# Attention and gated MLP on one core: later heads' scores in plain fp32 on half the array, p turned through DRAM

## The chip, the cores and the metric

The kernel runs on one core of a Trainium2 chip. The metric is the device time of one execution in microseconds; of several executions, the median. Engines are named as in the profile: PE is the tensor engine, DVE the vector engine, ACT the scalar engine, POOL GpSimd, SP the queue that issues most DMAs. PEld is PE's loading of weights.

## The reference

Banded attention with sink columns feeds a two-layer MLP with a cosine gate. Batch 4, 8 heads, 768 positions, head size 64; 3072 tokens of width 512, hidden width 2048. All in fp32.

```python
scores = scale * np.matmul(q, k.transpose(0, 1, 3, 2))
keep = is_sink | in_window                  # 4 sink columns, window 128
scores = np.where(keep, scores, -1000000000.0)
a = softmax(scores)                         # with 1e-9 in the denominator
x = np.matmul(a, v)                         # heads side by side: 3072 x 512
h = x @ w_in
out = (h * np.cos(h)) @ w_out
```

## The kernel before

The queries are cut into 12 chunks of 256 rows (two blocks of 128) of one batch, and a chunk has 8 heads. A query block needs the key block of its own rows and the one before, and 8 sink columns where it lies behind those (264 score columns in all). A chunk's attention output is the `x` of its MLP part: 8 slots per chunk, each with 24 matmuls at L458 (`h_mm`), the gate on ACT and DVE, and 12 matmuls at L518 (`out_mm`). Chunk 0 takes its second product in plain fp32 at L513. Elsewhere an fp32 operand is split in a rounded high part and a low part, both in the type fp32r, and the products hi\*lo, hi\*hi and lo\*hi are summed. The weights come as 64-bit floats and are put together on DVE early in the run (L579 to L621).

**Early heads** are the 24 heads of the first chunks of batches 0 to 2 (`NEH`). Their q and k are turned by PE (L862), the scores are plain fp32 matmuls with a pair of heads on the two halves of the rows (`scores_pe`, L882), p is turned by PE (`turn`, L1057), and the values are plain fp32 on the two halves of the columns (`values_pe`, L1110).

**Later heads** are the other 72 (64 of chunks behind a batch's first, 8 of batch 3's first). k is loaded twice, on partitions 0 to 63 and 64 to 127 (`load_k`, L813), and turned by DVE (`k_turn`, L911); the sink columns are appended (`k_sink`); k is split by `k_hi` (ACT, L923) and `k_lo` (DVE, L929), q by `q_hi` and `q_lo` (L898, L905) with the high part on one half of the partitions and the low part on the other. `scores` (L938) is two fp32r matmuls per head and query block, one with the high and one with the low part of k. `mask` (L951) moves the scores to SBUF with the mask added, then come exponential, `lap` (which folds the two key blocks), and `norm`. `turn` transposes p on PE (L1053, two 128x128 blocks; in batch 3's first chunk three, L1057); `p_hi` and `p_lo` split it (L1070, L1079), `part` on POOL separates the two key blocks again (L1092), and `values` multiplies (L1132).

PSUM has one bank `s` for scores and one `tp` for turns. At the start, the limits (window and sink count) come by ACT's queue, `limits` and `mask_0` to `mask_2` make three masks on DVE, and `beyond` tests whether the limits fit.

What sets the order: every step is entered in a `Plan` with the engines it may use, its estimated duration, the steps and buffers it waits for and a priority from the table `C`. `Plan.place` runs this list forward and back and fixes the engine and the place of each step; `emit` writes the instructions in that order, and each engine's queue keeps it. In gaps of PE before the first `out_mm`, `fill` puts matmuls on an unused tile (`idle`, L1411). So another number in `C` moves instructions all over the program.

Of the kernel before, what the change touches and what calls it, by code (L numbers as in the profile page):

```python
# [16 lines left out]
P = 128  # L17
# [10 lines left out]
C = {  # L28
# [7 lines left out]
}  # L36
TN, TV, TW = (230.0, 2.5), (128.0, 3.0), 1.7
BEGIN = {"PE": 3.4, "ACT": 0.7, "POOL": 2.6, "DVE": 2.3, "SP": 0.8}
MIN_TOP = 1.125 * 2.0**-15
# [11 lines left out]
class Plan:  # L51
# [12 lines left out]
    def __init__(self):  # L64
        self.steps, self.bufs, self.port, self.lock, self.hold, self.skew, self.more, self.trip = [], {}, set(), set(), set(), set(), {}, {}

# [5 lines left out]
    def add(self, engines, fn, deps, prio, table=None, port=False, lock=False, hold=True, more=0.0, skew=False, trip=1.7):  # L72
# [11 lines left out]
        self.more[i], self.trip[i] = more, trip  # L84
        return i

    def lap(self, i, e):
        return -0.025 if i in self.skew and e in ("ACT", "DVE") else self.OVERLAP[e]
# [144 lines left out]
def attn_moe_kernel(ctx, tc, q, k, v, n_sink, window, w_in, w_out, out):  # L233
# [45 lines left out]
    rel, col = rc[:, 0], rc[:, 1]  # L279
    nw_i = cp.tile([P, 2, 2], I32, name="nw_i")  # L280
# [9 lines left out]
    def setup():  # L290
# [17 lines left out]
        nc.vector.tensor_copy(out=rc, in_=rc_i)  # L308
        nc.vector.tensor_reduce(
# [4 lines left out]
    def load_limits(e):  # L314
        nc.scalar.dma_start(out=nw_i[:, 0, :], in_=n_sink.unsqueeze(0).broadcast_to([P, 2]))
        nc.scalar.dma_start(out=nw_i[:, 1, :], in_=window.unsqueeze(0).broadcast_to([P, 2]))
        nc.scalar.activation(out=flag[:, 2:3], in_=quarter[0:1], func=AF.Exp)

    def limits(e):
        nc.vector.tensor_copy(out=nw4, in_=nw_i)  # L320
        nc.vector.tensor_single_scalar(out=neg, in_=nw4[:, :, 0], scalar=0.0, op=ALU.is_lt)
# [4 lines left out]

    def beyond(e):
# [386 lines left out]
    def banded_path():  # L714
# [8 lines left out]
        diag, prev, cols = mb[:, SW:], mb[:, :P], ma[:, :P]  # L723
        vs = env.vs = ap.tile([P, H // GQ, GQ, 2, D], F32R, name="vs")
# [3 lines left out]
        def masked(m):  # L728
            nc.vector.tensor_scalar(out=m, in0=m, scalar1=-1.0, scalar2=MASKED, op0=ALU.add, op1=ALU.mult)

        def mask_0(e):
            nc.vector.tensor_scalar(out=diag, in0=rel, scalar1=wd_f, scalar2=None, op0=ALU.is_lt)
            nc.vector.scalar_tensor_tensor(out=diag, in0=rel, scalar=0.0, in1=diag, op0=ALU.is_ge, op1=ALU.mult)
            nc.vector.tensor_scalar(out=cols, in0=col, scalar1=ns_f, scalar2=None, op0=ALU.is_lt)
            nc.vector.tensor_tensor(out=m0, in0=cols, in1=diag, op=ALU.max)
            masked(m0)

        def mask_1(e):
            nc.vector.tensor_copy(out=mb[:, P:SW], in_=cols[:, :NSINK])
            nc.vector.tensor_scalar(out=prev, in0=rel, scalar1=float(P), scalar2=wd_f, op0=ALU.add, op1=ALU.is_lt)  # L740
            nc.vector.tensor_tensor(out=cols, in0=cols, in1=prev, op=ALU.max)
            nc.vector.tensor_copy(out=ma[:, P:], in_=diag)
            masked(ma)

        def mask_2(e):
            masked(mb)

        heads = []
        for a, (b, i0) in enumerate(chunks):
            for h in range(H):  # L750
# [12 lines left out]
                o.one = i0 > 0  # L763
                o.nw = [SW] * CB if o.one else o.w
# [5 lines left out]
        def load_batch_k(o):  # L770
            def fn(e):
                for dup in range(2):
                    for c in range(2):
                        nc.sync.dma_start(
                            out=o.xs[dup * 64 + c * 32 : dup * 64 + c * 32 + 32],
                            in_=k[o.b, :, 0:32, c * 32 : c * 32 + 32].rearrange("h s d -> s h d"),
# [12 lines left out]
        def batch_k(o):  # L789
            def fn(e):  # L790
                t = ap.tile([P, KB, SW], F32, name=f"tb_{o.tag}", tag="tk").rearrange("p n s -> p (n s)")[:, : H * 32]
                nc.vector.transpose(out=t, in_=o.xs.rearrange("p h s -> p (h s)"))
                o.ts = ap.tile([P, H, NSINK], F32, name=f"ts_{o.tag}", tag="ts")
# [840 lines left out]
```

## Time and profile before

| What | us |
|---|---|
| runs, median (lowest to highest, 3 runs) | 716.63 (716.15 to 719.03) |
| the profiled execution | 715.12 |
| its span | 713.4 |
| PE busy | 701.1 (98%) |
| DVE busy | 615.8 (86%) |
| ACT busy | 545.1 (76%) |
| POOL busy | 105.4 (15%) |

The span is from the first to the last instruction of the profiled execution, 1.7 us below its own time. The granted clock of PE is 1.00 in nearly the whole span. The DMA engines are busy 41% of it with the loads and stores of SP's queue. Busy time of PE counts a matmul from its start to its end, and matmuls overlap, so a group's sum of busy times may exceed the stretch that it takes.

### The profile page before, as it was taken

How to read it: one execution, taken by the hardware profiler on the slowest of the kernel's cores; microseconds unless marked ns; L12 is line 12 of the kernel's file. 1: busy time of each engine (PE TensorE's matmuls, PEld its weight loads, DVE VectorE, ACT ScalarE, POOL GpSimd, SP SyncE). 2: the span in 40 equal slices, each digit the busy share in tenths (PEclk: the TensorE clock that was granted, in tenths of full speed). 3: DMA queues.
4: the chain of work that ended last, by engine and by line, in shares of the span. 5: the costliest groups of instructions: out<-in, count | busy, mean ns of one | idle time of the engine just before them, and what ended most of it. 6: DMA issues, size and time to landing. Idle time of an engine off the chain costs nothing.

```text
span 713.4 us, 14956 instructions
## 1 busy us (share of the span) xinstructions
PE 701.1 (98%) x4780; PEld 622.7 (87%) x4780; DVE 615.8 (86%) x1766; ACT 545.1 (76%) x1349; POOL 105.4 (15%) x190
## 2 busy tenths in 40 slices
PE   8889999999999999999999999999999999999996
PEld 7676767989989999999999999999998999999995
DVE  7999999788999999999999998897798998875332
ACT  5989674488897988988978979878879788784431
POOL 1000000012122122221221221221010221212000
PEclk9999999999999999999999999999999999999999
DMA  6977762134644843843844532322332422100001
GB/s 171 255 230 218 216 181 66 30 50 124 176 95 99 216 104 87 227 104 61 226 93 102 122 52 47 77 40 48 84 53 47 86 50 40 47 12 8 31 1 33
DMA packets 215896, 71.48 MB, mean 100 GB/s; under 512 B 204288, under 2 KB 204800, under 8 KB 215808
## 3 DMA queue, kind: packets, MB, share of 16 engines
q1 hardware_dynamic: 215232, 70.17, 41.2%
q8 instruction: 40, 0.66, 0.4%
q14 instruction: 48, 0.39, 0.2%
q10 hardware_dynamic: 576, 0.26, 0.1%
HBM read 64.10 MB, written 6.29 MB: 99 GB/s over the span
## 4 chain that ended last, share of the span: by engine, by line
PE 93%; DVE 6%; issue 0%; ACT 0%; POOL 0%; POOLq 0%; DVEq 0%
PE h L458 38%; PE acc L518 34%; PE av L1132 6%; PE s L938 5%; PE acc L513 4%; PE tp L1053 2%; DVE p L951 1%; PE tp L1057 1%; DVE w_in L585 1%; PE av L1110 1%; DVE w_in L591 1%; PE s L882 1%; PE idle L1411 1%; DVE lo_in L621 1%; PE gp L1037 0%
## 5 line engine op out<-in xcount | busy, mean ns | idle before, releaser
L458 PE MATMUL h<-xhi,lo_in 128*128 128x256 f32 x768 | 224.6, 292 | 0.2 <-DVE g L491 0.2
L458 PE MATMUL h<-xlo,hi_in 128*128 128x256 f32 x768 | 217.0, 283 | 0.0
L458 PE MATMUL h<-xhi,hi_in 128*128 128x256 f32 x768 | 216.9, 282 | 0.0
L458 PEld LDWEIGHTS h<-xhi,lo_in 128*128 128x128 f32 x768 | 146.2, 190 | 6.2 <-issue 1.6
L458 PEld LDWEIGHTS h<-xhi,hi_in 128*128 128x128 f32 x768 | 146.4, 191 | 4.1 <-issue 1.7
L458 PEld LDWEIGHTS h<-xlo,hi_in 128*128 128x128 f32 x768 | 146.3, 190 | 0.0
L518 PE MATMUL acc<-hi_out,ghi 128*128 128x512 f32 x350 | 142.4, 407 | 0.0
L518 PE MATMUL acc<-lo_out,ghi 128*128 128x512 f32 x350 | 137.6, 393 | 0.0
L518 PE MATMUL acc<-hi_out,glo 128*128 128x512 f32 x350 | 137.3, 392 | 0.0
L1092 POOL TENSOR_SCALAR_AFFINE_SELECT pz<-pz 128x512 fp32r<-128x512 f32 x128 | 83.1, 649 | 249.3 <-DVE pz L1079 230.4
L467 ACT ACTIVATE yt<-h 128x512 int32<-128x512 f32 x96 | 57.3, 597 | 51.0 <-PE h L458 50.0
L960 ACT ACTIVATE p<-p,st 128x264 f32<-128x264 f32 (+1 forms) x192 | 93.2, 488 | 0.2
L473 DVE SCALAR_TENSOR_TENSOR r<-h,yt 128x512 f32<-128x512 f32 x96 | 65.3, 681 | 26.0 <-ACT yt L467 25.8
L480 ACT ACTIVATE r<-r,neg 128x512 f32<-128x512 f32 x96 | 69.6, 725 | 21.6 <-DVE r L473 20.9
L951 DVE CUSTOM_DVE_ANT_0 p<-s,mk 128x264 f32<-128x264 f32 (+2 forms) x168 | 68.1, 405 | 12.6 <-PE s L938 8.9
L518 PEld LDWEIGHTS acc<-hi_out,glo 128*128 128x128 f32 x350 | 65.8, 188 | 14.8
L518 PEld LDWEIGHTS acc<-hi_out,ghi 128*128 128x128 f32 x350 | 66.1, 189 | 7.3
L518 PEld LDWEIGHTS acc<-lo_out,ghi 128*128 128x128 f32 x350 | 66.2, 189 | 7.0
L485 DVE TENSOR_TENSOR h<-h,r 128x512 f32<-128x512 f32 x88 | 60.9, 692 | 11.4 <-ACT r L480 10.8
L503 DVE TENSOR_TENSOR glo<-h,ghi 128x512 fp32r<-128x512 f32 x88 | 59.9, 680 | 12.0 <-ACT ghi L497 11.7
L497 ACT CAST ghi<-h 128x512 fp32r<-128x512 f32 x88 | 51.5, 585 | 24.5 <-DVE h L485 18.4
L938 PE MATMUL s<-r,l 128*128 128x264 f32 (+2 forms) x288 | 59.6, 289 | 0.0
(139 smaller groups left out, 1239.6 us busy)
## 6 DMA issues: line engine op xcount, KB each, us to landing
raw<-in_moe_w_in_dram SPq DMA_DIRECT2D x32, 512.0 KB, 4.5
raw<-in_moe_w_out_dram SPq DMA_DIRECT2D x32, 512.0 KB, 4.2
xk<-in_k_dram SPq DMA_DIRECT2D x256, 48.0 KB, 2.0
v<-in_v_dram SPq DMA_DIRECT2D x64, 96.0 KB, 2.2
out_dram<-raw SPq DMA_DIRECT2D x22, 256.0 KB, 3.1
xq<-in_q_dram SPq DMA_DIRECT2D x144, 32.0 KB, 1.9
v<-in_v_dram SPq DMA_DIRECT2D x32, 64.0 KB, 3.6
xq<-in_q_dram SPq DMA_DIRECT2D x24, 64.0 KB, 3.7
```

Of the source, the lines that this page charges most:

```text
L458: nc.tensor.matmul(out=o.h[:, t, :], lhsT=w[:, fs], rhs=xx[:, c, :], start=(c == 0 and n == 0), stop=(c == NC - 1 and n == 2),)
L467: nc.scalar.activation(out=yt, in_=o.h, func=AF.Copy, scale=INV2PI, bias=0.25)
L473: nc.vector.scalar_tensor_tensor(out=o.r, in0=o.h, scalar=INV2PI, in1=yt, op0=ALU.mult, op1=ALU.subtract)
L480: nc.scalar.activation(out=o.r, in_=o.r, func=AF.Sin, scale=TWOPI_DOWN, bias=quarter)
L485: nc.vector.tensor_tensor(out=o.h, in0=o.h, in1=o.r, op=ALU.mult)
L497: nc.scalar.copy(out=o.ghi, in_=o.h)
L503: e.tensor_tensor(out=o.glo, in0=o.h, in1=f32(o.ghi), op=ALU.subtract)
L518: nc.tensor.matmul(out=x.acc[j], lhsT=gg[:, t, j * P : (j + 1) * P], rhs=w, start=(f == 0 and n == 0), stop=(f == NFT - 1 and n == 2), ski ...
L938: nc.tensor.matmul(out=o.s_ps[j][:, :w], lhsT=o.l[:, j * P : (j + 1) * P], rhs=r.rearrange("p n s -> p (n s)")[:, c0 : c0 + w], start=(n = ...
L951: nc.vector.tensor_tensor_reduce(out=o.p[:, j, :w], in0=o.s_ps[j][:, :w], in1=masks[min(o.i0 + j, 2)][:, :w], op0=ALU.add, op1=ALU.min, sc ...
L960: nc.scalar.activation(out=o.p[:, j, :w], in_=o.p[:, j, :w], func=AF.Exp, bias=o.lead.st[:, 0, o.nth, j : j + 1], scale=-1.0, accum_out=o. ...
L1092: nc.gpsimd.affine_select(out=env.pz4[:, :, :, n], in_=f32(env.pz4)[:, :, :, 0], pattern=[[0, 2], [0, CB], [sign, P]], compare_op=ALU.is_g ...
```

## The change

- **Scores of later heads**: `load_k` brings the k of two heads, one on each half of the partitions, once. `k_turn` and `q_turn` serve a pair; `k_hi`, `k_lo`, `q_hi`, `q_lo` are gone. `scores` is one plain fp32 matmul per head and query block, two heads on the two halves of the rows; the second head's scores go to the bank `tp`. The sink keys are loaded and turned per pair.
- **p of later heads**: `turn` is left to the early heads. `p_blocks` has DVE turn p within blocks of 32x32 into `wt`; `p_store` writes it to a DRAM tile `dt` in 4 DMAs, `p_load` reads it back in 4 DMAs, so that the blocks land where the full transpose wants them (`pt`). `p_hi` and `p_lo` read `pt` from SBUF, and `p_lo` may go to POOL.
- **Early values**: `values_pe` takes a pair of heads in one step, alternating the two halves.
- **Masks**: `mask_0` to `mask_2` compare with the limits as loaded and multiply by the mask value at once; `limits` is one cast, and `beyond` with the rest of the old `limits` goes behind the masks of a later head. The first k load is halved between SP and ACT's queue, and the copy of the first turned q and k is in two steps. The loads of the sink keys and values wait for masks of head 8 and head 12.
- **The table `C`** and the cost constants are other numbers.

```diff
-    "AE": 17.984, "ALT": 0.863, "CK": 42.675, "DA": 1.14, ...
+    "AE": 14.238, "ALT": 0.313, "CK": 66.775, "DA": -2.106, ...
...
         def load_k(o):
             def fn(e):
-                for dup in range(2):
+                for h in range(2):
                     for c in range(2):
                         nc.sync.dma_start(
-                            out=o.xk[dup * 64 + c * 32 : dup * 64 + c * 32 + 32],
-                            in_=k[o.b, o.h, o.kb0 * P : (o.kb0 + o.nkb) * P, c * 32 : c * 32 + 32].rearrange(
+                            out=o.xk[h * 64 + c * 32 : h * 64 + c * 32 + 32],
+                            in_=k[o.b, o.h + h, o.kb0 * P : (o.kb0 + o.nkb) * P, c * 32 : c * 32 + 32].rearrange(
...
-        def scores(o, j):
-            def fn(e):
-                i, w = o.i0 + j, o.w[j]
-                o.s_ps[j] = ps.tile([P, 2, NT], F32, name=f"s_{o.tag}_{j}", tag="s").rearrange("p a b -> p (a b)")
-                c0 = max(i - 1 - o.kb0, 0) * o.sw
-                for n, r in enumerate((o.r1, o.r2)):
+        def scores(o, o1, j):
+            def fn(e):
+                w = o.w[j]
+                sa = ps.tile([P, 2, NT], F32, name=f"s_{o.tag}_{j}", tag="s").rearrange("p a b -> p (a b)")
+                sb = ps.tile([P, 4 * P], F32, name=f"s_{o1.tag}_{j}", tag="tp")
+                c0 = max(o.i0 + j - 1 - o.kb0, 0) * o.sw
+                for n, (oo, s_ps) in enumerate(((o, sa), (o1, sb))):
+                    oo.s_ps[j] = s_ps
+                    r = slice(n * D, (n + 1) * D)
                     nc.tensor.matmul(
-                        out=o.s_ps[j][:, :w], lhsT=o.l[:, j * P : (j + 1) * P],
-                        rhs=r.rearrange("p n s -> p (n s)")[:, c0 : c0 + w], start=(n == 0), stop=(n == 1),
+                        out=s_ps[:, :w], lhsT=o.tq[r, j * P : (j + 1) * P],
+                        rhs=o.tk[r].rearrange("p n s -> p (n s)")[:, c0 : c0 + w], start=True, stop=True,
                     )
...
+        def p_blocks(o, oe):
+            def fn(e):
+                if o is oe:
+                    o.wt = ap.tile([P, 2 * (CB + 1) * P], F32, name=f"wt_{o.tag}", tag="wt", bufs=WT)
+                flat = oe.wt[:, o.odd * o.nb * P : (o.odd + 1) * o.nb * P]
+                if o.one:
+                    nc.vector.transpose(out=flat.rearrange("p (j w) -> p j w", j=CB), in_=o.p[:, :, :P])
+                    return
+                for j, c0 in enumerate((0, o.w[0])):
+                    nc.vector.transpose(out=flat[:, c0 : c0 + o.w[j]], in_=o.p[:, j, : o.w[j]])
+            return fn
+
+        def p_store(oe):
+            def fn(e):
+                n = 2 * oe.nb
+                oe.dt = dp.tile([32, 2 * (CB + 1) * 4, 4, 32], F32, name=f"dt_{oe.tag}", tag="dt", bufs=DT)
+                src = oe.wt[:, : n * P].rearrange("p (g b) -> p g b", b=32)
+                for r in range(4):
+                    nc.sync.dma_start(out=oe.dt[:, : n * 4, r], in_=src[r * 32 : r * 32 + 32])
+            return fn
+
+        def p_load(oe):
+            def fn(e):
+                n = 2 * oe.nb
+                oe.pt2 = ap.tile([P, 2 * (CB + 1) * P], F32, name=f"pt_{oe.tag}", tag="pt2", bufs=PT)
+                src = oe.dt.rearrange("a (g c) r b -> c a g (r b)", c=4)
+                dst = oe.pt2.rearrange("p (g w) -> p g w", w=P)
+                for c in range(4):
+                    nc.sync.dma_start(out=dst[c * 32 : c * 32 + 32, :n], in_=src[c, :, :n])
+            return fn
...
-        i = add([("ACT", 5.2)], load_limits, [], -3000.0)
-        i = add([("DVE", 0.76)], limits, [i], -3000.0)
-        add([("DVE", 0.4)], beyond, [i], C["LB"])
-        mks = [add([("DVE", 1.4)], mask_0, [i], -3000.0, port=True)]
-        mks.append(add([("DVE", 1.15)], mask_1, mks[:], -2999.0, port=True))
-        mks.append(add([("DVE", 0.3)], mask_2, mks[1:], C["LB"], port=True))
+        lim = i = add([("ACT", 4.13)], load_first, [], -3000.0, ahead=1.0)
+        i = add([("DVE", 0.2)], limits, [i], -3000.0)
+        read = i
+        mks = [add([("DVE", 0.58)], mask_0, [i], -3000.0, port=True)]
+        mks.append(add([("DVE", 0.78)], mask_1, mks[:], -2999.0, port=True))
+        mks.append(add([("DVE", 0.15)], mask_2, mks[1:], C["LB"], port=True))
...
+            ts = []
+            for oo in (oe, o):
+                ts.append(
+                    add([("DVE", dve(oo.nb * P) + (0.02 if oo.one else 0.1))], p_blocks(oo, oe), oo.nm + (ts or [bwt]), t + DA + C["TB"] + 0.1 * oo.odd)
+                )
+                oo.bp.users.append(ts[-1])
+            i = add(dma(2.0), p_store(oe), [*ts, bdt], t + DA + C["TB"] + 1.0, more=205.0 * o.nb, trip=1.9)
+            bwt.users.append(i)
+            o.rd = add(dma(2.0), p_load(oe), [i, o.bpt], t + DA + C["TB"] + 2.5, more=140.0 * o.nb, trip=1.9)
+            bdt.users.append(o.rd)
```

On PE, among the slots of the MLP, one head's scores before: two fp32r matmuls of 264 columns into one bank (`r` are the parts of k, `l` those of q).

```order
L458 MATMUL h_1885<-xhi_721,hi_in_1138 128x256
L458 MATMUL h_1885<-xlo_748,hi_in_1138 128x256
L938 MATMUL s_2_4_1_1922<-r_0_2_4_1867,l_2_4_1864 128x264
L938 MATMUL s_2_4_1_1922<-r_0_2_4_1873,l_2_4_1864 128x264
L458 MATMUL h_1885<-xhi_721,lo_in_1176 128x256
L458 MATMUL h_1885<-xhi_721,hi_in_1158 128x256
```

After, for the same query block, the pair's two heads, in plain fp32 from `tk` and `tq` as they were turned:

```order
L468 MATMUL h_1905<-xhi_744,hi_in_1206 128x256
L468 MATMUL h_1905<-xlo_870,hi_in_1206 128x256
L931 MATMUL s_2_4_1_1940<-tk_2_4_1640,tq_2_4_1642 128x264
L931 MATMUL s_2_5_1_1941<-tk_2_4_1640,tq_2_4_1642 128x264
L528 MATMUL acc_0_1597<-hi_out_1265,ghi_1777 128x512
L528 MATMUL acc_0_1597<-lo_out_1560,ghi_1777 128x512
```

Four matmuls for a pair and block have become two, and they stand as one block between full matmuls; there are 72 such blocks.

On PE before, the turn of a later head's p stood between matmuls at L518:

```order
L518 MATMUL acc_0_2227<-hi_out_1011,ghi_2321 128x512
L518 MATMUL acc_0_2227<-lo_out_1446,ghi_2321 128x512
L518 MATMUL acc_0_2227<-hi_out_1011,glo_2330 128x512
L1053 MATMUL tp_2_4_2450<-ident,p_2_4_1892 128x128 x2
L518 MATMUL acc_1_2237<-hi_out_1011,ghi_2321 128x512
L518 MATMUL acc_1_2237<-lo_out_1446,ghi_2321 128x512
```

The changed order has no such rows for later heads.

On SP before, in a later stage: k loads of one head (x4), q, v, and weights for the check.

```order
L813 DMA xk_75<-in_k_dram 32x12x32 x4
L801 DMA xq_74<-in_q_dram 32x8x32 x4
L813 DMA xk_76<-in_k_dram 32x12x32 x4
L824 DMA v_77<-in_v_dram 128x3x64
L639 DMA raw_71<-in_moe_w_out_dram 128x1024
L774 DMA xq_73<-in_k_dram 32x8x32 x4
```

After, around one pair's round trip: `dt` is the DRAM tile, `pt` what comes back.

```order
L1072 DMA dt_2_4_3763<-wt_2_4_3707 32x16x32 x4
L839 DMA v_77<-in_v_dram 128x3x64
L557 DMA out_dram<-raw_72 128x512
L839 DMA v_77<-in_v_dram 128x3x64
L649 DMA raw_71<-in_moe_w_in_dram 128x1024
L557 DMA out_dram<-raw_70 128x512
L1082 DMA pt_2_4_3848<-dt_2_4_3763 32x4x128 x4
```

The load of `pt` waits in this queue for the store of `dt` to land; between them stand what the plan put there, and what follows it waits too. A store's DMA has 32x16 pieces of 32 floats, a load's 32x4 of 128.

## Rows read from the trace of the kernel before

**Rows 1.** The page, busy time of each engine: us (share of span), instructions.

```profile
PE 701.1 (98%) x4780; PEld 622.7 (87%) x4780; DVE 615.8 (86%) x1766; ACT 545.1 (76%) x1349; POOL 105.4 (15%) x190
```

**Rows 2.** Busy us by stretch (with instructions), then clock, DMA share, GB/s.

```profile
20.00:60.00 40.00, 35.71 (x265) 26.75 (x265) 39.90 (x125) 35.65 (x103) 0.95 (x2) 1.00 0.86 241
60.00:100.00 40.00, 40.00 (x222) 27.05 (x222) 39.84 (x97) 31.29 (x76) 0.93 (x2) 1.00 0.79 221
200.00:300.00 100.00, 100.00 (x699) 92.15 (x698) 97.13 (x296) 87.79 (x224) 21.04 (x36) 1.00 0.59 140
```

**Rows 3.** Groups by shape, PE: count | busy us, mean ns | idle before.

```profile
L938 PE MATMUL s<-r,l 128*128 128x264 f32 x256 | 53.6, 291 | 0.0
...
L1053 PE MATMUL tp<-ident,p 128*128 128x128 f32 x128 | 24.4, 272 | 0.0
```

**Rows 4.** Timeline of PE, 306 to 308 us: start, us, line, operation, count.

```profile
306.37 0.40 PE L938 MATMUL s<-r,l 128*128 128x264 f32 x2
306.61 0.39 PE L518 MATMUL acc<-hi_out,ghi 128*128 128x512 f32 x1
...
307.30 0.38 PE L1053 MATMUL tp<-ident,p 128*128 128x128 f32 x2
307.44 0.36 PE L458 MATMUL h<-xhi,lo_in 128*128 128x256 f32 x1
307.64 0.28 PE L458 MATMUL h<-xhi,hi_in 128*128 128x256 f32 x1
```

**Rows 5.** Timeline of PE, 45.6 to 47.1 us, an early pair's scores.

```profile
45.67 0.28 PE L458 MATMUL h<-xhi,hi_in 128*128 128x256 f32 x1
45.79 0.28 PE L458 MATMUL h<-xlo,hi_in 128*128 128x256 f32 x1
46.00 0.37 PE L882 MATMUL s<-qks 64*128 64x128 f32 x1
46.01 0.37 PE L882 MATMUL qk<-qks 64*128 64x128 f32 x1
46.21 0.27 PE L882 MATMUL s<-qks 64*128 64x128 f32 x1
...
46.32 0.38 PE L882 MATMUL s<-qks 64*128 64x256 f32 x1
...
46.54 0.38 PE L882 MATMUL s<-qks 64*128 64x256 f32 x1
...
46.85 0.38 PE L410 MATMUL av<-xhi,gt 128*128 128x256 f32 x1
47.08 0.28 PE L458 MATMUL h<-xhi,lo_in 128*128 128x256 f32 x1
```

**Rows 6.** Timeline of PE, 94.3 to 94.9 us, a turn of three blocks.

```profile
94.38 0.49 PE L1057 MATMUL tp<-ident,p 128*128 128x128 f32 x3
94.62 0.36 PE L458 MATMUL h<-xhi,lo_in 128*128 128x256 f32 x1
94.83 0.28 PE L458 MATMUL h<-xhi,hi_in 128*128 128x256 f32 x1
```

**Rows 7.** Groups by shape, DVE.

```profile
L929 DVE TENSOR_TENSOR r<-tk,r 128x408 fp32r<-128x408 f32 x64 | 37.1, 579 | 1.3
...
L911 DVE STREAM_TRANSPOSE tk<-xk 128x384 f32<-128x384 f32 x64 | 36.4, 568 | 0.4
```

**Rows 8.** DMA issues by line: count, KB each, median us from issue to landing.

```profile
xk<-in_k_dram SPq DMA_DIRECT2D x256, 48.0 KB, 2.0
...
v<-in_v_dram SPq DMA_DIRECT2D x32, 64.0 KB, 3.6
```

**Rows 9.** Timeline of PE, 74.6 to 75.5 us, an early head's values alone.

```profile
74.62 0.86 PE L1110 MATMUL av<-firsts,v 128*64 128x256 f32 x4
75.41 0.70 PE L513 MATMUL acc<-w_out,g 128*128 128x512 f32 x1
```

**Rows 10.** Timeline of DVE at the first mask; in brackets, idle time and releaser.

```profile
9.23 0.29 DVE L951 CUSTOM_DVE_ANT_0 p<-s,mk 128x128 f32<-128x128 f32 x1 [0.80 <-PE qk L882]
```

More of the change, by code (lines that the diff above doesn't have):

```diff
@@ L70, in buf, with add @@
         return row[-1]
-    def add(self, engines, fn, deps, prio, table=None, port=False, lock=False, hold=True, more=0.0, skew=False, trip=1.7):
+    def add(self, engines, fn, deps, prio, table=None, port=False, lock=False, hold=True, more=0.0, skew=False, trip=1.7, ahead=0.0):
         i = len(self.steps)
@@ L83, in add @@
                 self.hold.add(i)
-        self.more[i], self.trip[i] = more, trip
+        self.more[i], self.trip[i], self.ahead[i] = more, trip, ahead
         return i
     def lap(self, i, e):
+        if self.ahead[i]:
+            return self.ahead[i]
         return -0.025 if i in self.skew and e in ("ACT", "DVE") else self.OVERLAP[e]
@@ L763, in banded_path @@
                 o.one = i0 > 0
+                o.nb = CB if o.one else o.n
                 o.nw = [SW] * CB if o.one else o.w
@@ L1051, in fn @@
                 n = 0
-                for j in range(CB if o.one else 0):
-                    nc.tensor.transpose(out=o.tp[:, j * P : (j + 1) * P], in_=o.p[:, j, :P], identity=ident)
-                for kb, qs in o.cols if not o.one else ():
+                for kb, qs in o.cols:
                     for i in qs:
@@ L1180, in before_softmax @@
                 first = o
-                bx, o.bt, btb, o.bv, o.bvs = buf("xq", 2), buf("ts", 1), buf("tk", 1), buf("xb", 1), buf("vs", 1)
+                bx, o.bt, btb, o.bv, o.bvs = buf("xq", 2), buf("ts", 1), buf("tk", TK), buf("xb", 1), buf("vs", 1)
                 o.xs = xq_ts[bx.nth]
-                i = add(dma(1.9), load_batch_k(o), [bx], t - 9.5 * T + DQ, more=205, trip=3.0)
+                i = add(dma(1.9), load_batch_k(o), [bx, *heads[H].msk], t - 9.5 * T + DQ, more=205, trip=3.0)
+                if g == NEH // H * H:
+                    add([("DVE", 0.85)], beyond, [read, *heads[H].msk], t - 7.5 * T)
                 o.kt = add([("DVE", dve(H * 32) + 0.25)], batch_k(o), [i, o.bt, btb], t - 7.5 * T)
@@ L1186, in before_softmax @@
                 btb.users.append(o.kt)
-                i = add(dma(2.8), load_batch_v(o), [o.bv], t - 3 * T, more=64)
+                i = add(dma(2.8), load_batch_v(o), [o.bv, *heads[H + H // 2].msk], t - 3 * T, more=64)
                 o.vt = add([("DVE", 1.92)], vs_parts(o), [i, o.bvs], t - T + 3.4, port=True)
@@ L1237, in before_softmax @@
                     first.bt.users.append(k1)
-                k2 = add((("ACT", act(kw)),), k_hi(o), [k1, b1], t - 6 * T + DQ + 1.6)
-                k3 = add((sub(kw)[0], ("DVE", dve(kw))), k_lo(o), [k2, b2], t - 6 * T + DQ + 2.0, port=True, lock=True)
-                btk.users += [k2, k3]
-                o.kr = [k3]
-            if o.odd == 0 and not o.early:
-                for oo in (o, heads[g + 1]):
-                    oo.bl = buf("l", C["L"])
-                    q1 = add([("ACT", act(NT))], q_hi(o, oo), [q0, oo.bl], t - 6 * T + DQ + 0.6, skew=oo is not o)
-                    oo.ql = add([("DVE", dve(NT))], q_lo(o, oo), [q1], t - 6 * T + DQ + 0.9, port=True, skew=True)
-                    btq.users += [q1, oo.ql]
+                o.scores = []
+                for j in range(CB):
+                    bs, bt = buf("s", 1), buf("tp", 1)
+                    c0 = add(
+                        [("PE", SP2)], scores(o, heads[g + 1], j), [q0, k1, bs, bt], t - 5 * T + DS + (3.25, 5.55)[j]
+                    )
+                    o.btq.users.append(c0)
+                    o.btk.users.append(c0)
+                    o.scores.append((c0, bs, bt))
             o.bp = buf("p", C["PB"])
@@ L1265, in before_softmax @@
                 else:
-                    bs = buf("s", 1)
-                    c0 = add([("PE", 0.255)], scores(o, j), [o.ql, *o.kr, bs], t - 5 * T + DS + (3.25, 5.55)[j])
-                    for bb in (o.bl, b1, b2):
-                        bb.users.append(c0)
+                    c0 = heads[g - o.odd].scores[j][0]
+                    bs = heads[g - o.odd].scores[j][1 + o.odd]
                 c1 = add(
@@ L1309, in after_softmax @@
                 o.vl = add(dma(1.0), load_v_pair(o, heads[g + 1]), o.bxs, t - 2 * T + DV + 3.2, more=TV[0], trip=TV[1])
-            elif not o.early:
-                bx = buf("v32", C["XV"])
-                o.bxv = bx
-                i = add(dma(0.74), load_v(o), [bx], t - 2 * T + DV + 3.2, more=96)
             if o.early:
```

217 lines of the change are left out of this document (117 added, 100 removed), and 14 rows, old and new, of the table C.

## Prediction

> **What bounds the kernel now.** I read the page's busy times first: PE is busy 701.1 of 713.4 us [rows 1]. Then the busy time by stretch: between 60 and 100 us PE is busy 40.00 of 40.00 us, between 200 and 300 us 100.00 of 100.00 [rows 2], and it goes on so to 700 us. Between 20 and 60 us it is not full (35.71 of 40, part of it `idle` fillers), while DVE is (39.90) [rows 2]. So from 60 us on the time is the sum of what PE has to issue; before that DVE feeds it, and at the end a tail of some 6 us is left alone by this change. DVE at 97.13 of 100 us is nearly full too, but in the list of waits PE waits for nobody between 60 and 700 us: work taken from DVE or ACT there is worth nothing now.
>
> A busy time hides what PE really pays, since its matmuls overlap: L938 has 256 rows of 291 ns, 53.6 us of union [rows 3]. I therefore price by starts, from the timeline: a block costs the time from its start to the next start, plus what it adds to the neighbours.
>
> **Scores, before.** A head's block of two fp32r matmuls of 264 columns starts at 306.37 and is followed at 306.61 [rows 4]: 0.24 to 0.25 us, and the next acc matmul shows no delay. 64 heads x 2 blocks x 0.245 = 31.4 us. The 8 later heads of batch 3's first chunk have blocks of 128 and 256 columns: about 0.12 + 0.24 each, 2.9 us. Together 34.3 us.
>
> **Scores, after.** A pair of heads shares a block: two plain fp32 matmuls, on rows 0 to 63 and 64 to 127. The early heads already do that, at L882, and one such block stands among fp32r matmuls [rows 5]. There the reader sees: the `s` and `qk` rows of one step start at 46.00 and 46.01, so the two halves of the array run beside each other; each matmul is two rows, so 256 columns cost 2 x 0.22 us (46.32 to 46.54) and 128 columns 2 x 0.11. The block as a whole takes from 46.00 to 46.85, 0.85 us, which is 0.19 more than its columns (0.66). The h matmul before it, at 45.79, keeps PE 0.21 us rather than the usual 0.12 (45.67 to 45.79), and the one behind, at 46.85, 0.23. So going to the halves and back costs 0.19 + 0.09 + 0.11 = about 0.39 us per block, apart from the columns. By the order of the changed kernel, the 72 later blocks stand alone, each with one column step, 50 of them between fp32r matmuls on both sides. A block of 264 columns is then 0.45 + 0.39 = 0.84 us: 64 x 0.84 = 53.8 us; the 4 of 256 columns 0.83 and the 4 of 128 columns 0.61, 5.8 us. Together 59.6 us, **25.3 us more**. The bounds: columns alone, 0.45 per block, would give 31.4 us in all (a gain of 3); halves that took turns would add 0.45 per block. I take 0.84, because its row is the same kind of block among the same neighbours.
>
> The Trainium skill (TensorEngine Tiling (Array Packing), Theoretical Speedup) gives up to 2x for a contracted dimension of 64 or less, and no price of a switch stands beside it; by that table alone the blocks would cost their columns and the kernel would come out near 695 us. The row decides against it, and the table is the base of the first rival.
>
> **Turns, before.** Two transposes of p start at 307.30, the h matmul behind them at 307.44, and that one keeps PE until 307.64, 0.20 rather than 0.12 [rows 4]: 0.14 + 0.08 = 0.22 us per head, 64 heads, 14.1 us. Heads of batch 3's first chunk have three: 94.38 to 94.62, and again 0.09 on the next [rows 6], 0.33 x 8 = 2.6 us. All of L1053 and these go: **16.7 us less**. PE is thus 8.6 us longer between 60 and 700 us.
>
> **What takes the turns' place, and the splits that go.** Per pair two DVE turns of 128x256 (a turn of 384 columns is 568 ns [rows 7], so some 0.4 us each), 4 stores and 4 loads on SP. DVE loses the k split (L929, 64 x 579 ns) and half of the k turns (L911, 32 x 568 ns) [rows 7], and the q split; in sum more than it gains, ACT loses its halves of both splits. I cost all of it at nothing: PE waits for neither now. The cover of the round trip: the first DMA of a store has 512 pieces of 128 B. A k load of 384 pieces of 128 B lands in 2.0 us, a busy-stage v load in 3.6 [rows 8]; with four issues at about 0.49 us each way is 4.0 to 5.6 us, and there and back 8 to 11. In the changed order, DVE has 6.5 to 17.9 us of work (median 12, each instruction at the mean of its group) between the second turn of a pair and the first low part that needs the load; only the last two pairs have less than 8, and the values of the last chunk are wanted when DVE is little used. So it is hidden, with little to spare: if the cover were 1 us short for each of 36 pairs, DVE and ACT would slip before PE does. On SP a load waits for its store's landing, and what is queued behind it (v, the next k and q, weight checks) waits as well; k issues fall by half, the round trip adds 8 per pair, so SP has some 140 more issues, about 70 us, over 600. PE's next need of that queue is buffered a pair ahead.
>
> The Trainium skill (DMA: Bandwidth & Descriptors, Specifications) says that transfers under 512 B are read, modified and written; the store's 128 B pieces are of that kind. No row here shows such a write to memory; it is the second rival's ground.
>
> **Early values.** A pair's values in one block run both column halves together; 10 of 12 pairs stand so already. Of the two that don't, one lies where PE is full: its second block starts at 74.62, the next matmul at 75.41 [rows 9], 0.79 us and some 0.1 on the neighbours: **0.9 us less**. The other lies where DVE sets the pace: nothing.
>
> **Start.** The masks lose several DVE operations, and half of the first k load goes out on ACT's queue. At 9.23 DVE had waited 0.80 us for the first scores [rows 10]; that wait is what an earlier k can give back: **0.8 us less**. The shorter masks then end well before. `beyond` and the sink loads move behind; nobody waits for them.
>
> **Sum.** 715.12 us of the profiled execution + 25.3 - 16.7 - 0.9 - 0.8 = 722.0. The median of the runs, 716.63, is 1.5 above the profiled execution; so **723.5 us**, 1.0% slower. About 0.5% (3.6 us) is what a measurement of this kernel can tell from no change.
>
> **Rivals.** (1) *The switch is cheap in the later stage*, and the kernel is faster. All L882 rows lie in the first 90 us and carry two column steps; with blocks of one step, among dense fp32r work, part of the price may hide under other loads of weights. At half, 0.20 us, it gives 72 x 0.20 = 14.4 back: 709; without any, 695. It decides at 0.30 us per block, where the sum is zero. Against it: the price on both neighbours is the same at every L882 block that waits for nothing. (2) *The round trip is late*: values wait, and p buffers with them. At a quarter to half a microsecond of PE per pair, 36 pairs give 9 to 18 us: 732.5 to 741.5. Against it stands the cover above. (3) *The early stage gives more*: DVE is full from 20 to 100 us [rows 2], and another order of weights, with fewer mask steps, might save 6 or 7 us rather than 0.8: about 717. Against it: the weights' own DVE work there is unchanged. (4) *The halves take turns*, so that the pairing isn't what it says: 72 x 0.45 = 32 us, 756; the two starts 0.01 us apart [rows 5] speak against it.
>
> **Chances.** Forecast 0.47 (its own range 719 to 728), (1) 0.27, (2) 0.13, (3) 0.10, (4) 0.03. The range from 705 to 733 leaves out the far part of (1), most of (2), and (4): about 0.2. Faster by over 0.5%: 0.22 of (1) and 0.02 of the rest, 0.24. Within 0.5%: the lower edge of the forecast 0.12, the upper edge of (1) 0.05, 0.08 of (3): 0.25. Slower: 0.51.
>
> **What would show it.** PE still full from about 60 to 700 us and waiting for nobody; no turn of p among the later heads; score blocks with both halves starting together and, from the matmul before to the one behind, some 0.84 us for 264 columns. If that stretch is under 0.7 us, rival 1 holds; if PE shows waits on the parts of p or on `pt` landings, rival 2; if the first full stretch of PE begins several us earlier, rival 3. A gain that comes from DVE's or ACT's relief in the middle would prove the reading of the bound wrong.

## The result and the profile after

The changed kernel takes **721.66 us** (median of 6 runs, 720.71 to 723.37) against 717.0 for the kernel before on the same chip. The ratio of the runs is 1.0075, interval 1.0061 to 1.0088, or 4.4 to 6.3 us slower. The forecast was 723.5. The profiled execution took 723.37 us, its span 721.6. The two profiled executions lie further apart than the medians, 8.25 us: that of the kernel before is 1.9 below its median on this chip, that of the changed kernel 1.7 above.

The page of the kernel after, busy time of each engine (answers to [rows 1]):

```profile
PE 709.4 (98%) x4655; PEld 596.8 (83%) x4655; DVE 570.0 (79%) x1687; ACT 497.3 (69%) x1207; POOL 87.7 (12%) x140
```

Busy us by stretch, after (answers to [rows 2]):

```profile
20.00:60.00 40.00, 38.32 (x287) 29.79 (x289) 39.83 (x120) 35.39 (x101) 0.00 (x0) 1.00 0.81 229
60.00:100.00 40.00, 40.00 (x238) 26.41 (x235) 38.91 (x103) 34.85 (x86) 0.00 (x0) 1.00 0.79 217
200.00:300.00 100.00, 99.20 (x665) 85.10 (x663) 87.80 (x279) 70.00 (x170) 18.99 (x28) 1.00 0.64 144
```

PE is 8.3 us busier (4.4 of it are fillers before 60 us, 16.5 us instead of 12.0), DVE has lost 46 us and ACT 48, and the time went with PE. Between 200 and 300 us DVE is down from 97.13 to 87.80 and PE is nearly as full as before. The 0.8 us missing there are PE's only wait between 60 and 705 us. The list of waits names `part` on POOL, and the timeline of DVE shows what stands behind it:

```profile
PE av L1159 <- POOL pz L1119: 0.8, 1, 0.8
```

```profile
253.55 0.70 DVE L644 CUSTOM_DVE_ANT_0 raw<-raw 128x512 f32<-128x512 f32 x1 [2.10 <-DMA raw<-in_moe_w_in_dram]
```

DVE waited for a piece of the weights to land (the check of the weights at L644); `p_lo` (254.17), `part` (254.72) and the values followed. No `pt` was late here, but the piece shares SP's queue with the round trip, so this wait doesn't clear the trip by itself. It belongs to this execution: the runs with no trip and with fewer fillers, in the same order, have no wait of PE there.

A later pair's scores in the timeline of PE (start, us, line, operation, count; answers to [rows 4, 5]):

```profile
303.55 0.28 PE L468 MATMUL h<-xhi,hi_in 128*128 128x256 f32 x1
303.67 0.28 PE L468 MATMUL h<-xlo,hi_in 128*128 128x256 f32 x1
303.88 0.71 PE L931 MATMUL s<-tk,tq 64*128 64x264 f32 x4
304.52 0.38 PE L1159 MATMUL av<-pz,vr 128*128 128x256 f32 x1
304.74 0.28 PE L1159 MATMUL av<-gt,vs 128*128 128x256 f32 x1
```

The h matmul ahead keeps PE 0.21 us instead of 0.12, the block 0.64, the matmul behind 0.22 instead of 0.12: 0.83. Over all 72 blocks the medians are 0.646 + 0.090 + 0.102 = 0.838 us for 264 columns, 0.826 for 256 and 0.616 for 128; 64 x 0.838 + 4 x 0.826 + 4 x 0.616 = 59.4 us, where the prediction had 59.6. Groups by shape of the kernel after (count | busy us, mean ns | idle before):

```profile
L931 PE MATMUL s<-tk,tq 64*128 64x264 f32 x256 | 45.8, 435 | 0.0
...
L1060 DVE STREAM_TRANSPOSE wt<-p 128x256 f32<-128x256 f32 x64 | 27.7, 434 | 0.1
...
L913 DVE STREAM_TRANSPOSE tk<-xk 128x384 f32<-128x384 f32 x32 | 17.9, 559 | 0.0
```

DVE's turns of p cost 434 ns (0.4 was taken), and there are half as many k turns as in [rows 7]. The start did not go as predicted (timelines of PE and DVE; answer to [rows 10]):

```profile
7.14 0.38 PE L877 MATMUL qk<-ident,xq 128*128 128x128 f32 x2
```

```profile
9.43 0.29 DVE L944 CUSTOM_DVE_ANT_0 p<-s,mk 128x128 f32<-128x128 f32 x1 [2.81 <-PE qk L898]
```

DVE's masks end early now and it waits 2.81 us, but the first scores are no earlier: 9.43 us against 9.23. (Both times hang on when PE comes to its full clock; see the run with fewer fillers.)

### The profile page after: what moved, and what is told of

Read it like the earlier page. It is cut to its first block, busy times and chain, and to the rows that moved or that the text cites. A ratio compares the mean times of both kernels' runs of the same rounds, so it can differ in the third digit from the quotient of the medians.

```text
span 721.6 us, 14506 instructions
## 1 busy us (share of the span) xinstructions
PE 709.4 (98%) x4655; PEld 596.8 (83%) x4655; DVE 570.0 (79%) x1687; ACT 497.3 (69%) x1207; POOL 87.7 (12%) x140
## 3 DMA queue, kind: packets, MB, share of 16 engines
HBM read 66.98 MB, written 16.25 MB: 115 GB/s over the span
## 4 chain that ended last, share of the span: by engine, by line
PE 93%; DVE 2%; ACT 2%; SPq 1%; issue 1%; POOL 0%; DMA 0%; POOLq 0%; DVEq 0%; ACTq 0%
PE h L468 37%; PE acc L528 35%; PE s L931 6%; PE av L1159 6%; PE acc L523 4%; PE av L1137 1%; PE tp L1048 1%; PE idle L1470 1%; PE s L898 1%; ACT p L953 1%; DVE p L944 1%; PE qk L877 1%; ACT p L976 0%; PE gp L1030 0%; SPq L816 0%
## 5 line engine op out<-in xcount | busy, mean ns | idle before, releaser
L528 PE MATMUL acc<-hi_out,ghi 128*128 128x512 f32 x350 | 145.6, 416 | 0.0
L1119 POOL TENSOR_SCALAR_AFFINE_SELECT pz<-pz 128x512 fp32r<-128x512 f32 x128 | 84.9, 664 | 434.8 <-DVE pz L1103 378.9
L528 PEld LDWEIGHTS acc<-hi_out,ghi 128*128 128x128 f32 x350 | 66.0, 189 | 20.8 <-issue 16.5
L944 DVE CUSTOM_DVE_ANT_0 p<-s,mk 128x264 f32<-128x264 f32 (+2 forms) x168 | 65.2, 408 | 20.5 <-PE s L931 16.8
L1159 PE MATMUL av<-pz,vr 128*64 128x128 f32 (+3 forms) x416 | 53.4, 245 | 0.8 <-POOL pz L1119 0.8
```

The lines of the kernel that those rows point to most:

```text
L528: nc.tensor.matmul(out=x.acc[j], lhsT=gg[:, t, j * P : (j + 1) * P], rhs=w, start=(f == 0 and n == 0), stop=(f == NFT - 1 and n == 2), ski ...
L944: nc.vector.tensor_tensor_reduce(out=o.p[:, j, :w], in0=o.s_ps[j][:, :w], in1=masks[min(o.i0 + j, 2)][:, :w], op0=ALU.add, op1=ALU.min, sc ...
L1119: nc.gpsimd.affine_select(out=env.pz4[:, :, :, n], in_=f32(env.pz4)[:, :, :, 0], pattern=[[0, 2], [0, CB], [sign, P]], compare_op=ALU.is_g ...
L1159: nc.tensor.matmul(out=dst, lhsT=lhs, rhs=rhs, start=(n == 0), stop=(n == len(seq) - 1), skip_group_check=True)
```

## The experiments

Ratios are to the kernel before, run beside each kernel. The changed kernel stands at 1.0075; a difference of 0.001 is 0.72 us.

### What a score block pays for

**The second pass.**

```diff
-                for n, (oo, s_ps) in enumerate(((o, sa), (o1, sb))):
+                for n, (oo, s_ps) in enumerate(((o, sa), (o1, sb)) * 2):
                     oo.s_ps[j] = s_ps
+                    n = n % 2
```

> Every later score block issues its two half-array matmuls a second time, into the same banks, in the same step; the order of everything else stays. If a block is columns (0.45 us) plus one price for going to the halves and back (0.39 us), the second pass costs its columns alone: 64 x 0.45 + 4 x 0.44 + 4 x 0.22 = 31 us, so about 753 us. If there is no price for the switch and half-array columns simply run at 0.84 us per 264, the second pass costs as much as the first: 59 us, about 781 us.

Measured: 752.45 us, ratio 1.0515 (1.0497 to 1.0532), 0.0440 or 31.5 us above the changed kernel. Its timeline of PE:

```profile
304.55 0.28 PE L468 MATMUL h<-xlo,hi_in 128*128 128x256 f32 x1
304.76 1.16 PE L932 MATMUL s<-tk,tq 64*128 64x264 f32 x8
305.85 0.39 PE L468 MATMUL h<-xhi,lo_in 128*128 128x256 f32 x1
306.07 0.28 PE L468 MATMUL h<-xhi,hi_in 128*128 128x256 f32 x1
```

0.21 ahead and 0.22 behind are what they were, the block is 1.09 instead of 0.64: the second pass costs its columns, 0.45, and no second entry. So 0.39 of a block's 0.84 is a fixed price per visit.

**The whole array.**

```diff
-                    r = slice(n * D, (n + 1) * D)
+                    r = slice(0, P)
```

> The later scores run on all 128 rows, one matmul after the other, still plain fp32 (each adds up the products of both heads of the pair, so the scores are not the reference's); the order stays. If the 0.39 us belongs to going to the halves, a pair's block is 2 x 0.45 = 0.90 us instead of 0.84: 64 x 0.06 less what the 8 shorter blocks save, about 3 us more, 725 us; with the 0.08 to 0.14 us that the turns of p cost their neighbours in the kernel before, up to 732. If the price belongs to plain fp32 among fp32r, it stays: 0.90 + 0.39, 31 us more, about 753 us.

Measured: 725.36 us, ratio 1.0123 (1.0107 to 1.0140), 3.4 us above the changed kernel. Its timeline of PE:

```profile
304.11 0.28 PE L468 MATMUL h<-xlo,hi_in 128*128 128x256 f32 x1
304.23 1.05 PE L931 MATMUL s<-tk,tq 128*128 128x264 f32 x4
304.92 0.47 PE L1159 MATMUL av<-pz,vr 128*128 128x256 f32 x1
305.23 0.28 PE L1159 MATMUL av<-gt,vs 128*128 128x256 f32 x1
```

The matmul ahead keeps its 0.12. The two matmuls take 0.69 + 0.19 (the row behind stands 0.31 instead of 0.12) = 0.88 us, which is four times 0.222: columns and nothing else. So the price belongs to the halves, not to plain fp32 among fp32r. Beside each other the two matmuls save 0.445 us and pay 0.39: the halves gain 0.05 us per block.

The Trainium skill (TensorEngine Tiling (Array Packing), Key Properties) says that changing the tiling mode drains the engine. The three places where a block loses time, ahead, inside and behind, agree with that; the page gives no price, and these two runs do.

**One visit per pair.** Both query blocks in one step; since four blocks of 264 columns need 32 more than two banks hold, a third bank and a short matmul take the rest.

```diff
-                for j in range(CB):
-                    bs, bt = buf("s", 1), buf("tp", 1)
+                bs, bt = buf("s", 1), buf("tp", 1)
+                bc = [buf("b3", 1)] if o.one else []
...
+                c0 = add([("PE", SP2)], scores(o, heads[g + 1]), [q0, k1, bs, bt, *bc], t - 5 * T + DS + 3.25)
...
+                                nc.tensor.matmul(
+                                    out=dst, lhsT=o.tq[:, j * P : (j + 1) * P], rhs=o.z, start=True, stop=True
+                                )
```

> The changed kernel with both score blocks of a pair in one step, so that PE goes to the halves once per pair instead of twice. The third PSUM bank is taken from the MLP (two banks rotate there), the last 16 columns of the second head's second block are a short matmul on all 128 rows against a tile with zeros in the other head's rows, and the table of order is new. If the 0.39 us is paid per visit, 36 x 0.39 = 14 us go and 32 short matmuls of some 0.12 us (an estimate: less than the 0.22 us of 256 columns) come, 4 us: about 711.5 us, 5 us below the kernel before. If the price hangs on the blocks or on their columns, nothing is saved: 721 to 725.

Measured: 718.98 us, ratio 1.0052 (1.0034 to 1.0070), 1.6 us below the changed kernel, with intervals that touch, and still above the kernel before. Its timeline of PE:

```profile
310.47 0.28 PE L469 MATMUL h<-xlo,hi_in 128*128 128x256 f32 x1
310.68 0.72 PE L956 MATMUL s<-tk,tq 64*128 64x264 f32 x4
...
311.76 0.40 PE L952 MATMUL s<-rest,tq 128*128 128x16 f32 x2
312.01 0.37 PE L1189 MATMUL av<-pz,vr 128*128 128x256 f32 x1
312.21 0.28 PE L1189 MATMUL av<-gt,vs 128*128 128x256 f32 x1
```

0.09 ahead, 1.08 + 0.25 inside, 0.08 behind: 1.50 us per pair instead of 2 x 0.84. The visit saved is there. But the short matmul costs 0.22 where 0.12 was allowed (1.50 less the 1.28 of the second-pass run): 36 x 0.39 - 32 x 0.22 = 7 us less on PE. Of these, 1.6 show in the time; PE lost 1.2 us in new waits between 60 and 700 us, and what the new order cost elsewhere wasn't separated.

### The turns and the trip

**Scores alone.**

```diff
-            if o.odd == 0:
-                return
-            oe = heads[g - 1]
-            bwt, bdt, o.bpt = buf("wt", WT), buf("dt", DT), buf("pt2", PT)
...
+            pt = buf("b3", 1)
+            p0 = add([("PE", (0.07 if o.one else 0.113) * n)], turn(o), o.nm + [pt], t + DA + 1.3, more=0.08)
```

> The changed kernel, but p of the later heads is turned by PE again as in the kernel before (in a PSUM bank of its own, so the MLP rotates over two banks there instead of three); no round trip. If the trip is free and PE's issue time is the bound, the 16.7 us of turns come back whole: 721.7 + 16.7, about 738 us, and PE stays full. If the round trip costs the changed kernel time of its own, less than that comes back: 733 us or below.

Measured: 737.2 us, ratio 1.0313 (1.0294 to 1.0332): 0.0238, 17.1 us above the changed kernel. The turns come back whole (its MLP rotates over two banks, but PE waits for nothing between 60 and 700 us), so the round trip costs the changed kernel nothing that shows.

**No trip.** `wt` gets the buffers of `pt` as well.

```diff
         def p_store(oe):
+            return lambda e: None
...
         def p_load(oe):
             def fn(e):
+                oe.pt2 = oe.wt
```

> The stores of p to DRAM and the loads back are left out, and the values read p as DVE's turn within blocks leaves it (so the attention output is not the reference's); order and everything else stay. If the round trip is hidden, the time stays within 1.5 us of 721.7, and PE waits for nothing new. If the trip is late by a quarter to half a microsecond per pair, or its 16 MB of traffic holds up other loads, the kernel gets faster by 3 us or more, to 718 or less.

Measured: 721.25 us, ratio 1.0078 (1.0056 to 1.0101): no difference, within some 2 us. The 10 MB that p adds each way (16.25 MB written to memory in all instead of 6.29), in pieces of 128 and 512 B, cost nothing that shows here.

**A longer trip.**

```diff
+                far = dp.tile([32, 2 * (CB + 1) * 4, 4, 32], F32, name=f"far_{oe.tag}", tag="far", bufs=DT)
+                nc.sync.dma_start(out=far[:, : n * 4], in_=oe.dt[:, : n * 4])
-                src = oe.dt.rearrange("a (g c) r b -> c a g (r b)", c=4)
+                src = far.rearrange("a (g c) r b -> c a g (r b)", c=4)
```

> The changed kernel with one more leg in the round trip: p is copied from its DRAM tile to a second one before the loads read it, 4 to 5 us later; order and all else stay. With a cover of 6.5 to 17.9 us (median 12) against 8 to 11 of the trip, the longer trip of 12 to 16 us is late for about half of the pairs: PE waits for parts of p or their banks, and the kernel is 5 to 20 us slower. If the cover is much longer than read from the order, or the buffers of p take it up, the time stays within 2 us of 721.7.

Measured: 765.0 us, ratio 1.0698 (1.0678 to 1.0717), 45 us above the changed kernel, more than twice the expected upper end. Three stretches (columns as in [rows 2]), a wait of ACT and one of PE (us in total, times, longest) of this kernel:

```profile
200.00:300.00 100.00, 90.70 (x562) 76.11 (x560) 74.39 (x240) 61.35 (x150) 15.66 (x23) 0.93 0.57 135
300.00:400.00 100.00, 89.99 (x569) 75.87 (x566) 72.29 (x225) 62.64 (x157) 17.07 (x27) 0.97 0.63 156
...
500.00:600.00 100.00, 92.48 (x588) 78.40 (x587) 70.34 (x214) 64.92 (x159) 6.50 (x10) 0.98 0.49 106
```

```profile
ACT pz L1097 <- DMA pt<-far: 34.8, 19, 4.2
```

```profile
PE av L1161 <- POOL pz L1121: 15.7, 8, 3.3
```

ACT waits for `pt`, 1.8 us at a time; what stands behind p in its queue is late with it, and DVE, POOL and PE follow. "Hidden, with little to spare" was right, and a leg more turns it into the second rival. Not all of the 45 us are waits: PE loses 28.7 us between 200 and 700, and behind six of its waits its granted clock falls to half (1.2 GHz) for a while. By the clocks 0.93, 0.97 and 0.98 of these stretches that is some 12 us more (an estimate: 7 + 3 + 2), which an expectation of waits alone leaves out.

**DVE's load given back.**

```diff
                 nc.vector.transpose(out=o.tk[:, :, :P], ...)
+                for n in range(2):
+                    nc.vector.tensor_tensor(out=o.xk, in0=o.xk, in1=o.xk, op=ALU.mult)
```

> The changed kernel with two more DVE multiplications of 128x384 behind each later pair's k turn (on the loaded k, which nobody reads any more), some 36 x 2 x 0.55 = 40 us, about as much DVE time as the change took off in sum; the order stays. If PE's issue time is the bound and DVE's relief is worth nothing, the time stays within 2 us of 721.7, with DVE near 97 of 100 us between 200 and 400. If the relief is what lets the round trip fit, PE waits behind DVE and the kernel is 5 us slower or more.

Measured: 726.36 us, ratio 1.0157 (1.0135 to 1.0179), 5.9 us above the changed kernel. A stretch of it:

```profile
300.00:400.00 100.00, 98.64 (x648) 83.88 (x647) 93.60 (x282) 69.88 (x173) 17.26 (x27) 1.00 0.66 160
```

As the second expectation had it: DVE is busy 604 us instead of 570 (34 came, not 40), no more than 94 of 100 in the middle, and PE already loses 1.4 us there. Between 60 and 700 us PE's waits are 2.8 us, on `glo` of DVE, `part` of POOL and an `x` of DVE. So the relief doesn't make the kernel faster, but part of it is room that this order uses; that the round trip is what needs the room isn't shown by this run.

**The trip alone.** Scores in fp32r as before, and p through DVE and DRAM.

```diff
+            i = add(dma(2.0), p_store(oe), [*ts, bdt], ...)
+            o.rd = add(dma(2.0), p_load(oe), [i, o.bpt], ...)
+            if o.one:
+                p1 = add([("ACT", act(o.nb * P) + 0.005)], high, [od.rd, bhi, blo], t + DA + 1.8)
+                p2 = add(sub(o.nb * P), p_lo(o), [p1], t + DA + 2.3, port=True, lock=True)
```

> The kernel before with its fp32r scores, but p of the 64 heads with two turned blocks goes through DVE and DRAM as in the change (the 8 heads of batch 3's first chunk keep PE's turns), and the table of order is new. If PE's issue time is the bound and DVE's load does not matter, 64 x 0.22 = 14.1 us go: about 702.5 us. If DVE, at 97 of 100 us between 200 and 300 in the kernel before, is the next bound, its 64 x 0.434 = 28 us of added turns, less what POOL takes over, make PE wait: 710 to 730 us, and PE's waits name DVE, ACT or POOL tiles.

Measured: 744.06 us, ratio 1.0402 (1.0370 to 1.0433). A stretch and the longest wait of PE:

```profile
200.00:300.00 100.00, 93.48 (x619) 84.61 (x618) 82.58 (x228) 73.92 (x181) 62.54 (x93) 0.97 0.63 142
```

```profile
PE h L459 <- DVE glo L504: 9.5, 7, 3.5
```

PE has 14 us less to issue and waits 23 us between 60 and 700, though no engine is full: POOL took over much of the splitting (388 us busy instead of 105).

**The trip with fewer k turns.**

```diff
+                    k2 = add((("ACT", act(kw)),), k_hi(o, oo, True), [k1, oo.b1], ...)
+                    k3 = add((("ACT", act(kw)),), k_hi(o, oo, False), [k2], ...)
+                    k4 = add((sub(kw)[0], ("DVE", dve(kw))), k_lo(o, oo), [k2, oo.b2], ...)
```

> The changed kernel with fp32r scores again, and the round trip for the 64 heads with two turned blocks (8 heads use PE's turns): k is loaded and turned once per pair, ACT writes k's high part on both halves of the rows, DVE or POOL the low part on one half (the other half keeps what an earlier head left there), so DVE carries less than in the trip alone; the table of order is new. If PE's issue time is all that counts, 716.6 less 14.1 us of turns: about 702.5. If three engines that are all 75 to 90 per cent full can't be kept in step by a fixed order, as in the run of the trip alone, PE waits for DVE, ACT and POOL: 715 to 740.

Measured: 734.2 us, ratio 1.0256 (1.0236 to 1.0276). Between 200 and 300 us:

```profile
200.00:300.00 100.00, 92.70 (x627) 82.70 (x628) 89.04 (x254) 81.24 (x194) 34.77 (x60) 1.00 0.56 130
```

Better than the trip alone, but PE loses 18.6 us between 200 and 600 us. ACT waits 8.9 us for landings of `pt`.

**The trip for late heads only.**

```diff
+                o.trip = o.one and len(heads) >= LATE
...
+            if not o.trip:
+                return o.tp[:, :NT]
```

> The kernel before, with its fp32r scores and its k and q loads, but the last 40 of its 96 heads send p through DVE and DRAM; the heads before them, whose stage has DVE at 97 of 100 us, keep PE's turns. The planner counts a longer trip than in the trip alone (3.0 us for each way instead of 1.9), and the table of order is new. If PE's issue time is the bound and DVE has room behind 350 us (90 of 100 us and less there, and 40 x 0.434 = 17 us come), 40 x 0.22 = 8.8 us go: about 708, up to 712 if the new order loses some us in the early stage. If DVE, ACT and a transfer in one chain can't be kept in step in this stage either, PE waits there and the time is 717 us or more.

Measured: 722.32 us, ratio 1.0097 (1.0071 to 1.0122). Of the last 40 heads, 8 are of batch 3's first chunk and keep PE's turns, so 32 x 0.22 = 7.0 us could go. Three stretches:

```profile
20.00:60.00 40.00, 34.05 (x264) 26.71 (x260) 38.21 (x120) 34.06 (x99) 0.00 (x0) 1.00 0.85 239
...
400.00:500.00 100.00, 99.33 (x685) 90.31 (x684) 94.12 (x279) 85.09 (x215) 27.09 (x45) 1.00 0.49 101
500.00:600.00 100.00, 98.94 (x682) 90.33 (x681) 92.02 (x265) 82.60 (x210) 16.87 (x34) 1.00 0.42 83
```

The turns of DVE for the trip stand from 375 to 638 us, and there the trip nearly fits: PE stays at 98.9 and 99.3 of 100 with DVE at 92 to 94. Most of the loss is elsewhere: the 289th h matmul starts at 135.7 us against 129.3 (its neighbours lie up to 9.4 us behind), so the new table lost 6 us or more in the early stage; the last one starts 3.5 us late, so some 3 us or more came back; and the tail behind it is 2.7 us longer. An order that keeps the early stage of the kernel before and trips late was not made, and no kernel here beats the one before.

### The early stage

**Fewer fillers.**

```diff
+                gap = m
-                while start[i] - t > C["GAP"]:
+                while start[i] - t > C["GAP"] and (gap or m < 11):
```

> In the first gap of PE 11 filler matmuls instead of 18, as many as the kernel before has there. If the fillers are what holds the first turn of q back, it starts at about 6.1 us instead of 7.14, the first mask at about 8.4 to 8.7 us instead of 9.43, and the time falls by 0.5 to 1 us, to about 721. If the data come late, PE idles before the turn, the first mask stays at 9.4 us, and the time stays.

Measured: 722.21 us, ratio 1.0088 (1.0071 to 1.0105): no gain. Timelines of its PE and DVE:

```profile
6.08 0.63 PE L878 MATMUL qk<-ident,xq 128*128 128x128 f32 x2
6.50 0.63 PE L878 MATMUL qk<-ident,xk 128*128 128x128 f32 x2
```

```profile
8.88 0.29 DVE L945 CUSTOM_DVE_ANT_0 p<-s,mk 128x128 f32<-128x128 f32 x1 [2.25 <-PE qk L899]
```

The fillers did hold the turn back, 6.08 against 7.14 us. But the turns now stand 0.42 us apart instead of 0.22, and the first mask gains 0.55 us over the changed kernel's profile and 0.07 over that of the run without the trip (8.95), which has the same start with 18 fillers.

Such single profiles don't compare as they stand. Fillers stand 0.21 us apart at first and 0.12 later: PE starts at half clock (1.2 GHz) and comes to the full one (2.4 GHz) at a moment that differs from execution to execution. In the seven profiles with 18 fillers and this start the trace's first record of the full clock stands at 4.9, 5.5, 5.7, 5.9, 6.1, 6.6 (the changed kernel) and 7.9 us, and the first mask at 8.67, 8.95, 9.03, 9.13, 9.20, 9.43 and 10.03. Here the full clock comes at 8.0 us. Against its nearest neighbour, the profile with DVE's load given back, fewer fillers bring the first mask 1.15 us earlier:

```profile
10.03 0.29 DVE L946 CUSTOM_DVE_ANT_0 p<-s,mk 128x128 f32<-128x128 f32 x1 [3.40 <-PE qk L898]
```

That is what was expected. And the early stage passes it on: in all eight the 72nd h matmul starts 41.7 us behind the first mask. In the runs' times no gain shows, but these intervals can hardly tell the 0.5 to 1 us that were expected.

**The early part alone.**

```diff
+                y0 = add([("PE", VP * o.n)], values_pe(oe, o, x), [oe.p1, p1, i, x.bav], t + DA + 4.0)
...
+        mks = [add([("DVE", 0.58)], mask_0, [i], -3000.0, port=True)]
```

> The kernel before with the early part of the change alone: the remade masks and limits, the first k load halved over two queues, the copy of the first turned q and k in two steps, and the values of an early pair in one block; later heads and the table of order as before. By the prediction's terms 0.9 + 0.8 us go: 714.9 us. If the early stage gives more, as the third rival has it, 6 to 7 us go: about 710. If DVE's own weight work sets the early stage and nothing else does, the time stays: 716.6.

Measured: 717.56 us, ratio 1.0046 (1.0026 to 1.0065): 2 to 5 us slower, which neither side had. Two stretches, the fillers among its groups, and PE's longest waits between 60 and 100 us:

```profile
20.00:60.00 40.00, 36.46 (x274) 28.61 (x274) 39.58 (x122) 35.20 (x98) 1.20 (x2) 1.00 0.76 218
60.00:100.00 40.00, 38.56 (x234) 26.73 (x234) 39.84 (x99) 36.67 (x91) 1.20 (x2) 1.00 0.80 224
```

```profile
L1439 PE MATMUL idle<-gt 128*128 128x256 f32 x107 | 17.0, 301 | 0.1
```

```profile
PE tp L1069 <- ACT p L995: 0.9, 1, 0.9
PE tp L1069 <- ACT firsts L455: 0.5, 1, 0.5
```

The paired values save PE 1.6 us, two blocks of 0.80 (14 blocks become 12), and the fillers grow from 65 rows to 107, while PE is no longer full between 60 and 100 us: it waits for `p` and `firsts` from ACT. DVE is as full as before (39.58 and 39.84 of 40). The steps are new and the table is that of the kernel before, so the order is another one, not made for these steps; whether the part itself or this order costs the 2 to 5 us isn't shown.

## Why the prediction was right, and where not

**The bound.** PE is full from 60 to 700 us before and after, and the time follows what it issues. This carried the forecast, and the runs with the scores doubled (31 expected, 31.5 measured), whole (3 and 3.4) and with PE's turns (16.7 and 17.1) came out on it.

**Scores, +25.3.** 59.4 us against the 59.6 forecast. The side before was a little too low: a block of two matmuls of 128 columns takes 0.17 us and 0.05 on the next, not 0.12, so 24.5 rather than 25.3 by the rows. In the time, the run with the scores alone, whose early part and table are changed too, stands 21.1 to 23.8 us above the kernel before; 25.3 - 0.9 - 0.8 would be 23.6. One early block read with its neighbours [rows 5] was worth more than the busy time of its group; the price didn't hide in the later stage, so the first rival fell (0.838, where it needed under 0.7). The halves start 7 ns apart, so the fourth fell.

**Turns, -16.7.** Confirmed by the run with the scores alone.

**The round trip and the relief at nothing.** Right for the trip in this kernel, and the second rival fell: without it the time is the same. That work taken from DVE or ACT "is worth nothing now" was too flat: 34 us given back to DVE cost 5.9, and with the fp32r scores the full trip did not fit in the two orders that were made. Whether another order would fit it is open.

**Early values -0.9 and start -0.8.** The values stand in the trace as priced: the two split pairs are gone, one of them where PE was full. The start failed as it was put. An earlier k did not bring the first mask earlier, since 18 fillers stand ahead of the turns where 11 stood, and the clock decides how long those take: the kernel before had its full clock from 7.3 us and its first mask at 9.23, while the changed kernel's profiles with the full clock at 6.6 and 7.9 us have it at 9.43 and 10.03. At like clock the start is later by some 0.5 us (an estimate between the two). Nor did another part of the early stage make up for it: between 20 and 60 us PE is busy 38.32 us instead of 35.71, but 7.15 of it instead of 4.46 are fillers, so the other matmuls are the same 31.2 us. The third rival has no support there. The fillers alone, before and after:

```profile
20.00:60.00 40.00, 4.46 (x27) 1.00 0.86 241
20.00:60.00 40.00, 7.15 (x43) 1.00 0.81 229
```

**How near the number came.** Scores and turns make +8.6 by the prediction and 7.8 by the rows. The profiled executions differ by 8.25, the runs by 4.4 to 6.3. The 2 to 4 us between are not in the rows. They are about as large as the distances of the two profiled executions from their medians together (1.9 and 1.7), and their cause stays open. That the forecast, which took off 0.8 us for a start that did not come, lies within 2 us of the median is in part luck.

## What to carry to other kernels

Going to half of the array and back is paid per visit, so price it by a block with its neighbours in the trace and put what can share the halves into one visit; an isolated pair of matmuls hardly gains (0.05 us here). Relief of an engine that nobody waits for isn't worth time, but it is room that another part can need: before splitting a change, see which part fills what the other empties. A transfer that is hidden with little to spare should be tested with a longer one: here one leg more cost 45 us, some 12 of them by a lower clock behind PE's waits. And what happens in the first microseconds should be compared at the same moment of full clock, not by one profile of each kernel.

## What was not expected of the hardware

Plain fp32 on the whole array stands among fp32r matmuls at the price of its columns: 0.222 us per 264 columns and pass, 0.69 of the 0.88 in the block and 0.19 on the matmul behind, nothing on the one ahead. The turns on PE leave 0.08 of their 0.22 us on the next one in the same way [rows 4]. A plain fp32 matmul of 16 columns adds 0.22 us in its two passes, where the two passes of 264 columns take 0.44. Behind one half-array block stands a plain fp32 turn (L1030), and the way back costs it 0.03 instead of 0.10; there is only one such place. The moment at which PE comes to its full clock ranged from 4.9 to 7.9 us in seven profiles with one and the same start, and moved the first mask by 1.4 us.
